# The second layer's order written out by hand, without arithmetic on GpSimd and with its weight units fetched sixteen ahead

## The chip, the cores and the metric

The kernel runs on one core of one Trainium2 chip. The metric is the device time of one execution in microseconds (us), as the median of several executions.

The names used below are those of the profile: PE is TensorE, DVE is VectorE, ACT is ScalarE, POOL is GpSimd, SP is SyncE, whose queue issues most DMAs.

## What is computed

Memory attention over 4 batches of 576 tokens and 8 heads (softmax over the sequence, 32 memory slots), then two feed-forward layers over the 2304 tokens. The change touches the border between the two layers and all of the second one.

```python
def _moe_ref(x, w_in, w_out):            # first layer: 512 -> 2048 -> 512
    h = np.maximum(x @ w_in, 0.0)
    return (h * h @ w_out).astype(np.float32)

def _moe2_ref(x, w_in, w_out):           # second layer: 512 -> 2048 -> 512
    h = x @ w_in
    sp = np.where(h > 20.0, h, np.log1p(np.exp(np.minimum(h, 20.0))))
    g = h * np.tanh(sp)                  # "mish"
    return (g @ w_out).astype(np.float32)

def reference(**kwargs):
    ...
    x = np.ascontiguousarray(attn_out.transpose(0, 2, 1, 3)).reshape(B * S, H * D)
    x = _moe_ref(x=x, **moe_kwargs)
    return _moe2_ref(x=x, **moe2_kwargs)
```

## The kernel before

**Arithmetic.** Each float32 operand is split in a high part (a cast to fp32r on ACT) and a low part (the rest, by a subtraction on DVE), and a product is three matmuls: high by high, low by high, high by low. The second layer's two products are done 2 by 2 in blocks with seven block products instead of eight, which needs sums of blocks on both sides: sums of weights, made once and stored in DRAM as "units" (`wf`, 256 KB each), and sums of activations, made beside the matmuls.

**Weight sums.** The class `Fold` makes the units out of the raw weights. For each 128 rows an exponent step on ACT (L275, Prelu) and two bit steps on DVE (L291, L293; `fields`) rebuild the float32 number; for each pair of row groups seven steps (`pair`) make sums on DVE, a cast on ACT (L310), a subtraction on DVE (L311) and a write from POOL's queue to `wf` (L312). The staging buffers of these writes come from `fold.stage`. This goes on beside the first layer, a step or two at each call of `fold.tick`, and the last nine casts run beside the first steps of the second layer, one at each step, with five staging buffers (three in the pool `cv`, two in `cs`).

**Border.** The last tile of the first layer (`a_tile`, L241 to L629) runs its second matmul group (`mm2_step`, L568 to L570) three steps late. After it, `flush()` makes the last `g` operand (cast L622 and subtraction L623 on DVE) and `run_pend(0)` runs the last three such groups, then copies the sums out (L585, L587) and stores them.

**Second layer.** Tokens go in three groups of 768. In each group there are 56 "h" steps (`h_step`: 8 row groups `k` by 7 products `j`) and 56 "b" steps (`b_step`: 7 products by 8 `k`); each is six matmuls of 384 columns that use one unit. In an h step, PSUM goes to SBUF by a copy on ACT (j=0) or an add on DVE (L1034, L1042, L1045), and Mish runs on ACT (L1030). For the b steps `cast_step` makes the high part (ACT, L1068) and the low part (DVE, L1069) of the operand, three steps ahead. Three sums are made on POOL: two for the operands (L1071, L1073, 128x384, 48 in all) and the sums of the next group's input (L918, L922, L925, L928 in `y_work`, 128x768, four for each of two groups). Four loads of the next group's input (L904) are at h steps 8 to 14.

**Units.** `feed` issues the loads of units from SP, in order. Unit n goes to one of 8 buffers, so that it can be issued once unit n-8 has been used; from unit 56 on there are 16 buffers.

**Order.** The tile framework orders each engine's instructions by its own estimate of times, within the dependences and within a few orderings given by hand (`behind`, L141). So DVE, ACT and PE mix steps of the second layer with the end of the first one, and POOL's sums go where the planner puts them.

Of the kernel before, what the change touches and what calls it, by code (L numbers as in the profile page):

```python
# [38 lines left out]
def body(tc, q, kvm, kvt, phi, w_in1, w_out1, w_in2, w_out2, out):  # L39
# [108 lines left out]

    class Conv:
# [86 lines left out]
    class Fold:  # L236
# [32 lines left out]

        def work(self, start, pops):  # L270
            todo, self.bits = self.bits, []
            if start and self.started < self.loaded and len(self.steps) < 5 and self.landed():
                key, u = self.order[self.started]
                high = self.raw[key, u][:, :, 1].bitcast(F32)
                nc.scalar.activation(high, high, AF.Prelu, scale=2.0 ** -112, alpha=-2.0 ** 32)  # L275
                self.started += 1
                self.bits.append((key, u))
# [618 lines left out]
    def y_work(i, raw, tmp):  # L896
# [16 lines left out]
        sub = nc.vector.tensor_sub if i == 0 else nc.gpsimd.tensor_sub  # L913
# [13 lines left out]
        def sum4():  # L927
            sub(r[1, 0], r[1, 0], r["t2"])  # L928
# [4 lines left out]
        if i:  # L933
# [3 lines left out]
                lambda: cast(2, r[0, 1]), lambda: (cast(4, r[1, 0]), sum4()),  # L937
# [40 lines left out]
    assert not y0  # L978
    flush()
    run_pend(0)  # L980
# [31 lines left out]
    def h_step(i, k, j, banks, tmp, g):  # L1012
# [7 lines left out]
        for d in range(2):  # L1020
# [5 lines left out]
            nc.tensor.matmul(ps, wl, yh[:, d], start=False, stop=end, **kw)  # L1026

# [4 lines left out]
        def total(name, a):  # L1032
            t = half_tile("hs", f"hs{m}", 3)
# [3 lines left out]
        if j == 0:  # L1037
            tmp["t"] = half_tile("ht", f"ht{m}", 2)
            nc.scalar.copy(tmp["t"], ps)
        elif j == 1:  # L1040
            tmp["u2"] = half_tile("hu2", f"hu2{m}", 2)
            add(tmp["u2"], tmp["t"], ps)  # L1042
        elif j == 2:
            tmp["u3"] = half_tile("hu3", f"hu3{m}", 2)
# [19 lines left out]
    def cast_step(j, k, g):  # L1064
        x = g[k, OPER[j]]
        hi, lo = ops[j, k] = tuple(
            G.tile([P, HT], F32R, tag=f"op{part}", name=f"op{part}{now}", bufs=5) for part in "hl")
        marks["hi"] = nc.scalar.copy(hi, x)  # L1068
        marks["lo"] = sub(lo, x, hi.bitcast(F32))  # L1069
        if j == 0:  # L1070
            at(k, lambda: nc.gpsimd.tensor_sub(x, g[k, "x1"], x))  # L1071
        elif j == 4:
            at(k, lambda: nc.gpsimd.tensor_sub(x, x, g[k, "a11"]))  # L1073

    def b_step(i, j, k, banks, tmp):
# [8 lines left out]
        for d in range(2):  # L1084
            ps = banks[role][d][:, :HT]
            wh, wl = (w[:, s, d * P:d * P + P] for s in range(2))
            first, end = k == 0 and j < 4, k == NPG - 1
            nc.tensor.matmul(ps, wh, hi, start=first, stop=False, **kw)  # L1088
            nc.tensor.matmul(ps, wl, hi, start=False, stop=False, **kw)  # L1089
            nc.tensor.matmul(ps, wh, lo, start=False, stop=end, **kw)  # L1090
        if k < NPG - 1:
            return

        def each(f, *ts, of=role):
            for d in range(2):
                f(*(t[:, d] for t in ts), banks[of][d][:, :HT])
# [4 lines left out]
        def store(t, a, b):  # L1101
            c0 = i * TT + a * HT
            nc.sync.dma_start(
                out[b * 256:b * 256 + 256, c0:c0 + HT].rearrange("(d p) t -> p d t", p=P), t)

        if j == 0:
            tmp["t"] = big("bt")
            each(nc.scalar.copy, tmp["t"])
        elif j == 1:
            tmp["u2"] = big("bu2")  # L1110
# [101 lines left out]
```

## Time and profile before

| | us |
|---|---|
| median of 3 executions | 760.62 (760.58 to 760.94) |
| profiled execution | 760.09 |
| its span, first to last instruction | 758.3 |
| first matmul of the second layer | 381.25 |
| last matmul's start | 754.04 |

The profile is one execution on the one core. Times of rows are in us from the span's start. PE is pipelined: a matmul of 384 columns is shown with about 0.34 us and the next one starts 0.174 us later, so the distance between starts tells the pace.

### The profile page before, as it was taken

To read this page: it belongs to the slowest core of one execution; us is meant where nothing else is said; L and a number is where in the kernel's file an instruction comes from. 1 tells how busy PE (TensorE), PEld (TensorE's weight loads), DVE (VectorE), ACT (ScalarE), POOL (GpSimd) and SP (SyncE) were. 2 spreads that over 40 slices of the span, in tenths; PEclk is the share of its full clock that TensorE was granted. 3 is DMA by queue.
4 is the path that set the end of the run, shared out by engine and by line. 5 is a ranking of instruction groups with operands and counts; after the bars stand their busy time and mean duration, and the time that the engine had idled before them with its cause. 6 is when DMAs were issued, how large, how long until landed. Compare 5 with 4: busy or idle time off the path is not lost. (4 is left out here: it accounts for less than half of the span.)

```text
span 758.3 us, 15324 instructions
## 1 busy us (share of the span) xinstructions
PE 728.6 (96%) x5480; PEld 691.1 (91%) x5480; DVE 529.9 (70%) x1072; ACT 425.1 (56%) x960; POOL 131.1 (17%) x176
## 2 busy tenths in 40 slices
PE   5699999999999999999998999999999999999997
PEld 4487898999888898999998999989999989999997
DVE  3979936436697779778979746884746794656584
ACT  3677856656558587766845435652334652334552
POOL 0000000001112123233225201230411050111040
PEclk8699999999999999999999999999999999999999
DMA  9994704107888779679879889888987888787882
GB/s 336 404 409 171 246 32 140 56 30 257 315 310 310 272 280 332 230 273 303 298 254 365 277 259 355 253 251 277 332 270 251 251 256 286 242 265 237 267 263 83
DMA packets 87756, 195.27 MB, mean 258 GB/s; under 512 B 9856, under 2 KB 21120, under 8 KB 87680
## 3 DMA queue, kind: packets, MB, share of 16 engines
q1 hardware_dynamic: 78720, 164.92, 65.0%
q0 software_dynamic: 8960, 29.37, 9.9%
q8 instruction: 44, 0.72, 0.4%
q14 instruction: 32, 0.26, 0.1%
HBM read 151.26 MB, written 42.99 MB: 256 GB/s over the span
## 5 line engine op out<-in xcount | busy, mean ns | idle before, releaser
L568 PE MATMUL a<-g,o1h 128*128 128x288 f32 x512 | 149.2, 299 | 0.7 <-ACT g L620 0.5
L569 PE MATMUL a<-g,o1l 128*128 128x288 f32 x512 | 148.4, 297 | 0.0
L570 PE MATMUL a<-g,o1h 128*128 128x288 f32 x512 | 132.2, 295 | 0.1
L1069 DVE TENSOR_TENSOR opl<-a,oph 128x384 fp32r<-128x384 f32 x144 | 92.9, 664 | 44.4 <-ACT oph L1068 43.8
L1024 PE MATMUL hb<-ych,u 128*128 128x384 f32 x336 | 113.8, 339 | 3.2 <-DVE hs L1034 1.8
L1025 PE MATMUL hb<-ycl,u 128*128 128x384 f32 x336 | 113.7, 338 | 0.0
L1026 PE MATMUL hb<-ych,u 128*128 128x384 f32 x336 | 110.9, 338 | 0.0
L1068 ACT CAST oph<-a 128x384 fp32r<-128x384 f32 x144 | 73.9, 513 | 61.2 <-PE b22acc L1089 8.0
L568 PEld LDWEIGHTS a<-g,o1h 128*128 128x128 f32 x512 | 96.3, 189 | 5.2 <-ACT s L614 2.1
L569 PEld LDWEIGHTS a<-g,o1l 128*128 128x128 f32 x512 | 96.5, 189 | 0.8 <-issue 0.8
L614 ACT ACTIVATE s<-h 128x288 f32<-128x288 f32 x128 | 52.7, 411 | 74.0 <-PE h L608 66.9
L570 PEld LDWEIGHTS a<-g,o1h 128*128 128x128 f32 x512 | 89.7, 188 | 3.8 <-issue 1.5
L1030 ACT ACTIVATE a<-hs 128x384 f32<-128x384 f32 x72 | 37.6, 525 | 98.1 <-DVE hs L1034 98.1
L606 PE MATMUL h<-ah,wp 128*128 128x288 f32 x256 | 78.9, 309 | 4.8 <-ACT wp L497 2.8
L623 DVE TENSOR_TENSOR g<-s,g 128x288 fp32r<-128x288 f32 x128 | 57.7, 451 | 34.6 <-ACT g L620 33.2
L312 POOL DMA_DIRECT2D wf_i<-st x56 | 30.7, 550 | 272.6 <-DVE st L311 257.1
L608 PE MATMUL h<-ah,wp 128*128 128x288 f32 x256 | 76.1, 297 | 0.7 <-DVE wp L498 0.7
L607 PE MATMUL h<-al,wp 128*128 128x288 f32 x256 | 76.4, 299 | 0.3 <-DVE al L481 0.3
L1034 DVE TENSOR_TENSOR hs<-hu,hb 128x384 f32<-128x384 f32 x72 | 39.6, 552 | 42.9 <-PE hb L1026 42.5
L1024 PEld LDWEIGHTS hb<-ych,u 128*128 128x128 f32 x336 | 63.6, 189 | 3.8 <-DVE hs L1034 2.1
L1025 PEld LDWEIGHTS hb<-ycl,u 128*128 128x128 f32 x336 | 63.5, 189 | 0.0
L1026 PEld LDWEIGHTS hb<-ych,u 128*128 128x128 f32 x336 | 63.4, 189 | 0.0
(277 smaller groups left out, 1559.1 us busy)
## 6 DMA issues: line engine op xcount, KB each, us to landing
u<-wf_i SPq DMA_DIRECT2D x168, 256.0 KB, 3.9
u<-wf_o SPq DMA_DIRECT2D x168, 256.0 KB, 3.3
raw_i<-in_moe_w_in_dram SPq DMA_DIRECT2D x32, 512.0 KB, 5.6
raw_o<-in_moe_w_out_dram SPq DMA_DIRECT2D x32, 512.0 KB, 6.8
wf_i<-st POOLq DMA_DIRECT2D x56, 256.0 KB, 4.8
wf_o<-st POOLq DMA_DIRECT2D x56, 256.0 KB, 4.6
win1r<-w_i SPq DMA_DIRECT2D x16, 512.0 KB, 5.3
kv<-in_kvm_dram SPq DMA_DIRECT2D x5, 1024.0 KB, 8.7
```

Of the source, the lines that this page charges most:

```text
L568: nc.tensor.matmul(o, wh[:, c, cs], sh, start=first, stop=False)
L569: nc.tensor.matmul(o, wl[:, c, cs], sh, start=False, stop=False)
L570: nc.tensor.matmul(o, wh[:, c, cs], sl, start=False, stop=last)
L606: nc.tensor.matmul(ph, w[:, 0, hg, fs], hi[:, hg], start=(hg == 0), stop=False)
L607: nc.tensor.matmul(ph, w[:, 0, hg, fs], lo[:, hg], start=False, stop=False)
L608: nc.tensor.matmul(ph, w[:, 1, hg, fs], hi[:, hg], start=False, stop=(hg == 1))
L623: marks["lo"] = nc.vector.tensor_sub(sl, s, sh.bitcast(F32))
L1024: nc.tensor.matmul(ps, wh, yh[:, d], start=(j < 4 and d == 0), stop=False, **kw)
L1025: nc.tensor.matmul(ps, wh, yl[:, d], start=False, stop=False, **kw)
L1026: nc.tensor.matmul(ps, wl, yh[:, d], start=False, stop=end, **kw)
L1068: marks["hi"] = nc.scalar.copy(hi, x)
L1069: marks["lo"] = sub(lo, x, hi.bitcast(F32))
```

## The change

A context manager `written` is added. Between its entry, just before the `flush()` at the border, and its exit after the last step, every instruction of PE, DVE and ACT is put behind the one traced before it on the same engine. So these three engines follow the order of the source. SP's and POOL's queues are not bound by it. In that order:

- All outstanding exponent steps (L275) and the load of Mish's activation table come first on ACT, then the rest of the first layer, then the h steps. The two bit steps that are left run at steps 3 and 5, and the pending steps of `pair` at every second step from step 7 on. The two extra staging buffers (`cs`) are gone, so these writes share three.
- Units 16 to 23, 32 to 39 and so on use eight more buffers (`ru2`); `feed` runs at the end of a step and goes up to 16 units ahead from step 16 on, two units at each step from 8 to 15.
- In the first group the loads of the next input are at steps 22 to 28 and its sums at 34, 39 and 44.
- Sums on POOL go to DVE: `x2` (in the h steps) and `x4` (`FOURTHS`), and `y_work`'s four sums.
- Temporaries share one tag `w` of 13 buffers; casts run four steps ahead in place of three; casts of the next input sit at `CASTS`.
- At the end of a b product each half is copied out and stored by itself (128 rows), the first half before the matmuls of the second.

```diff
+    @contextlib.contextmanager
+    def written(*engines):
+        traced = nc.cur_bb.bb.instructions
+        last = {x.engine: x for x in traced}
+        seen = traced[-1]
+        yield
+        start = next(k for k in reversed(range(len(traced))) if traced[k] is seen) + 1
+        for x in traced[start:]:
+            if x.engine not in engines:
+                continue
+            if x.engine in last:
+                tc.add_manual_dep(
+                    x, last[x.engine].name,
+                    mybir.DependencyInfo(mybir.DependencyClass.NoSync, mybir.DependencyReason.DATA),
+                    reason="written")
+            last[x.engine] = x
...
+        def start(self):
+            key, u = self.order[self.started]
+            high = self.raw[key, u][:, :, 1].bitcast(F32)
+            nc.scalar.activation(high, high, AF.Prelu, scale=2.0 ** -112, alpha=-2.0 ** 32)
+            self.started += 1
+            self.bits.append((key, u))
...
-        sub = nc.vector.tensor_sub if i == 0 else nc.gpsimd.tensor_sub
+        sub = nc.vector.tensor_sub
...
-            pool, tag = (G, "ru2") if n >= 56 and n % 2 else (Y2, "ru")
+            pool, tag = (G, "ru2") if n >= 16 and n // 8 % 2 == 0 else (Y2, "ru")
...
+    layer2 = written(mybir.EngineType.PE, mybir.EngineType.DVE, mybir.EngineType.Activation)
+    layer2.__enter__()
     flush()
+    extra[0] = None
+    while fold.started < fold.cap:
+        fold.start()
+    nc.scalar.preload_act_table_set("mish")
+    late, fold.bits = fold.bits, []
     run_pend(0)
...
-    cm_cs, CS = open_pool("cs", "right")
-    def stage_cs(n):
-        pool, tag, bufs = (CS, "stg2", 2) if n % 5 in (1, 3) else (CV, "stg", 3)
-        return pool.tile([P, 2, 256], F32R, tag=tag, name=f"st{n}", bufs=bufs)
-    fold.stage = stage_cs
...
+            def second():
+                g[k, "x2"] = half_tile(f"x2_{k}", f"x2{i}{k}", 1)
+                sub(g[k, "x2"], g[k, "x1"], g[k, "a11"])
             at(3, sums)
+            at(5, second)
-    OPER = ["a11", "a11", "a21", "x1", "a12", "a22", "a12"]
+    OPER = ["a11", "x2", "a21", "x1", "a12", "a22", "x4"]
...
-        if j == 0:
-            at(k, lambda: nc.gpsimd.tensor_sub(x, g[k, "x1"], x))
-        elif j == 4:
-            at(k, lambda: nc.gpsimd.tensor_sub(x, x, g[k, "a11"]))
+    def fourth(k, g):
+        x = g[k, "x4"] = g.pop((k, "a11"))
+        sub(x, g[k, "a12"], g[k, "x2"])
...
-    AHEAD = 3
+    AHEAD = 4
+    CASTS = (4, 10, 15, 20, 22, 27, 36, 42)
+    FOURTHS = (7, 12, 17, 25, 29, 38, 40, 44)
...
     for now, (kind, i, one, two) in enumerate(plan):
-        feed(now + (8 if now < 56 else 16))
...
+        if kind == "h":
+            if i == 0 and late and step in (3, 5):
+                fold.fields(*late.pop(0))
+            elif i == 0 and fold.steps and step > 6 and step % 2:
+                assert step < 40
+                fold.steps.pop(0)()
+            if step == 0 and more:
+                loads, sums, casts = y_work(i + 1, in_g("yr", 4), in_g("yt", 2))
+            if more and step in ((22, 24, 26, 28) if i == 0 else (8, 10, 12, 14)):
+                loads.pop(0)()
+            if more and step in ((34, 39, 44) if i == 0 else (24, 29, 34)):
+                sums.pop(0)()
+        else:
+            if more and step in CASTS:
+                casts.pop(0)()
+            if step in FOURTHS:
+                fourth(FOURTHS.index(step), g)
+        next(part, None)
+        feed(now + 9 if now < 8 else min(now + 17, 2 * now + 2))
+    layer2.__exit__(None, None, None)
```

## Rows read from the trace of the kernel before

**Rows 1.** The page, part 1: busy time (share of the span) and instructions by engine.

```profile
PE 728.6 (96%) x5480; PEld 691.1 (91%) x5480; DVE 529.9 (70%) x1072; ACT 425.1 (56%) x960; POOL 131.1 (17%) x176
```

**Rows 2.** Busy time by window; after POOL: granted PE clock, DMA share, GB/s.

```profile
410.00:420.00 10.00, 6.81 (x32) 6.17 (x32) 10.00 (x14) 3.24 (x7) 7.26 (x9) 0.90 1.03 400
```

**Rows 3.** Waits of PE in the b steps: who for whom, us in total, times, longest.

```profile
PE b02acc L1090 <- DVE opl L1069: 1.0, 2, 0.5
PE b12acc L1090 <- DVE opl L1069: 1.0, 2, 0.5
```

**Rows 4.** Timeline of PE in the first h steps: start, duration, instruction, idle before.

```profile
410.86 0.34 PE L1026 MATMUL hb<-ych,u 128*128 128x384 f32 x1
412.62 0.44 PE L1024 MATMUL hb<-ych,u 128*128 128x384 f32 x1 [1.42 <-DMA u<-wf_i]
...
415.70 0.34 PE L1026 MATMUL hb<-ych,u 128*128 128x384 f32 x1
417.80 0.48 PE L1024 MATMUL hb<-ych,u 128*128 128x384 f32 x1 [1.77 <-DVE hs L1034]
...
421.56 0.34 PE L1024 MATMUL hb<-ych,u 128*128 128x384 f32 x1
```

**Rows 5.** Timelines of DVE and POOL ahead of the second of these gaps.

```profile
411.61 3.76 DVE L1058 TENSOR_TENSOR a<-a,a 128x384 f32<-128x384 f32 x1
...
411.33 1.83 POOL L922 TENSOR_TENSOR yt<-yr,yt 128x768 f32<-128x768 f32 x1
413.10 1.85 POOL L925 TENSOR_TENSOR yr<-yr,yr 128x768 f32<-128x768 f32 x1
```

**Rows 6.** Timelines of PE and DVE in the first group's b steps.

```profile
494.35 0.41 PE L1090 MATMUL b00mm<-opl,u 128*128 128x384 f32 x1
...
501.61 0.34 PE L1088 MATMUL b02acc<-oph,u 128*128 128x384 f32 x1
...
493.72 5.23 DVE L1069 TENSOR_TENSOR opl<-a,oph 128x384 fp32r<-128x384 f32 x4
```

**Rows 7.** Timelines of PE and DVE at the border of the layers.

```profile
381.25 0.34 PE L1024 MATMUL hb<-ych,u 128*128 128x384 f32 x1
...
390.81 0.34 PE L1025 MATMUL hb<-ycl,u 128*128 128x384 f32 x1
...
394.57 0.29 PE L570 MATMUL a<-g,o1h 128*128 128x288 f32 x1
394.70 0.34 PE L1026 MATMUL hb<-ych,u 128*128 128x384 f32 x1
...
390.41 0.45 DVE L623 TENSOR_TENSOR g<-s,g 128x288 fp32r<-128x288 f32 x1
```

**Rows 8.** DMA issues, median us to landing: first two from 398 to 418, last from 425.

```profile
u<-wf_i SPq DMA_DIRECT2D x16, 256.0 KB, 5.9
wf_o<-st POOLq DMA_DIRECT2D x6, 256.0 KB, 5.8
...
u<-wf_i SPq DMA_DIRECT2D x22, 256.0 KB, 3.1
```

**Rows 9.** One weight sum's cast, subtraction and write; a short DVE sum; all writes' landing, 398 to 425.

```profile
398.70 0.41 ACT L310 CAST st<-ct_o 128x256 fp32r<-128x256 f32 x1 [3.38 <-DMA y<-ys]
399.14 0.42 DVE L311 TENSOR_TENSOR st<-ct_o,st 128x256 fp32r<-128x256 f32 x1 [2.92 <-ACT st L310]
399.86 0.54 POOL L312 DMA_DIRECT2D wf_o<-st  x1 [4.97 <-DVE st L311]
407.69 0.55 DVE L1057 TENSOR_TENSOR x<-a,a 128x384 f32<-128x384 f32 x1
...
DMA to landing us min/median/max: 2.8/5.6/6.2
```

**Rows 10.** Timeline at the end of the span: DVE's last two adds.

```profile
753.89 1.08 DVE L1096 TENSOR_TENSOR bo<-bu,b23acc 128x384 f32<-128x384 f32 x2 [3.74 <-PE b23acc L1090]
```

More of the change, by code (lines that the diff above doesn't have):

```diff
@@ L272, in work @@
             if start and self.started < self.loaded and len(self.steps) < 5 and self.landed():
[L273 to L277, printed above, removed]
+                self.start()
             for key, u in todo:
@@ L927, in sum4 @@
         def sum4():
-            sub(r[1, 0], r[1, 0], r["t2"])
+            if i:
+                sub(r[0, 0], r[1, 0], r["t2"])
+                r[1, 0] = r[0, 0]
+            else:
+                sub(r[1, 0], r[1, 0], r["t2"])
         sum1 = t1, lambda: cast(0, r[0, 0])
@@ L936, in y_work @@
             return work, sums, last + [
-                lambda: cast(2, r[0, 1]), lambda: (cast(4, r[1, 0]), sum4()),
+                lambda: cast(2, r[0, 1]), lambda: cast(4, r[1, 0]), sum4,
                 lambda: cast(6, r[1, 1]), lambda: cast(5, r[1, 0])]
@@ L1066, in cast_step @@
         hi, lo = ops[j, k] = tuple(
-            G.tile([P, HT], F32R, tag=f"op{part}", name=f"op{part}{now}", bufs=5) for part in "hl")
+            G.tile([P, HT], F32R, tag="w", name=f"op{part}{now}", bufs=13) for part in "hl")
         marks["hi"] = nc.scalar.copy(hi, x)
         marks["lo"] = sub(lo, x, hi.bitcast(F32))
-        if j == 0:
-            at(k, lambda: nc.gpsimd.tensor_sub(x, g[k, "x1"], x))
-        elif j == 4:
-            at(k, lambda: nc.gpsimd.tensor_sub(x, x, g[k, "a11"]))
+    def fourth(k, g):
+        x = g[k, "x4"] = g.pop((k, "a11"))
+        sub(x, g[k, "a12"], g[k, "x2"])
     def b_step(i, j, k, banks, tmp):
@@ L1083, in b_step, with big, store @@
         kw = dict(skip_group_check=True)
+        ends = k == NPG - 1
+        def big(tag, bufs=1):
+            return big_pool[0].tile([P, 2, HT], F32, tag=tag, name=f"{tag}{m}", bufs=bufs)
+        def store(t, d, a, b):
+            c0 = i * TT + a * HT
+            r0 = b * 256 + d * P
+            nc.sync.dma_start(out[r0:r0 + P, c0:c0 + HT], t[:, d])
+        if ends and j in (0, 1, 2):
+            tmp[j] = big(("bt", "bu2", "bu3")[j])
+        if ends and j in (2, 4, 5, 6):
+            t = big("bo", 3)
         for d in range(2):
@@ L1086, in b_step @@
             wh, wl = (w[:, s, d * P:d * P + P] for s in range(2))
-            first, end = k == 0 and j < 4, k == NPG - 1
+            first = k == 0 and j < 4
             nc.tensor.matmul(ps, wh, hi, start=first, stop=False, **kw)
             nc.tensor.matmul(ps, wl, hi, start=False, stop=False, **kw)
[L1090 to L1096, printed above, removed]
-        def big(tag, bufs=1):
-            return big_pool[0].tile([P, 2, HT], F32, tag=tag, name=f"{tag}{m}", bufs=bufs)
[L1101 to L1110, printed above, removed]
-            each(add, tmp["u2"], tmp["t"])
-        elif j != 3:
-            t = big("bo", 3)
+            nc.tensor.matmul(ps, wh, lo, start=False, stop=ends, **kw)
+            if d == 0:
+                yield
+            if not ends or j == 3:
+                continue
+            if j == 0:
+                nc.scalar.copy(tmp[0][:, d], ps)
+            elif j in (1, 2):
+                add(tmp[j][:, d], tmp[j - 1][:, d], ps)
             if j == 2:
-                tmp["u3"] = big("bu3")
-                each(add, tmp["u3"], tmp["u2"])
-                each(add, t, tmp["u3"], of=3)
+                add(t[:, d], tmp[2][:, d], banks[3][d][:, :HT])
             elif j == 4:
-                each(nc.scalar.copy, t)
-            else:
-                each(add, t, tmp["u2"])
-            store(t, *{2: (1, 1), 4: (0, 0), 5: (1, 0), 6: (0, 1)}[j])
+                nc.scalar.copy(t[:, d], ps)
+            elif j in (5, 6):
+                add(t[:, d], tmp[1][:, d], ps)
+            if j in (2, 4, 5, 6):
+                store(t, d, *{2: (1, 1), 4: (0, 0), 5: (1, 0), 6: (0, 1)}[j])
     plan = []
@@ L1138, in body @@
         if kind == "h":
-            h_step(i, one, two, banks, tmp, g)
-            if i == 0 and fold.busy():
-                assert step < 40
-                fold.tick(pops=1, took=0.43)
-            if step == 0 and more:
-                loads, sums, casts = y_work(i + 1, in_g("yr", 4), in_g("yt", 2))
-            if more and 8 <= step < 16 and step % 2 == 0:
-                loads.pop(0)()
-            if more and step in (24, 29, 34):
-                sums.pop(0)()
+            part = h_step(i, one, two, banks, tmp, g)
         else:
             if now == 56:
-                close(cm_cs)
                 close(cm_cv)
                 cm_bo, big_pool[0] = open_pool("bo", "right")
-            b_step(i, one, two, banks, tmp)
-            if more and 18 <= step < 46 and step % 4 == 2:
-                casts.pop(0)()
+            part = b_step(i, one, two, banks, tmp)
+        next(part)
         run_queue()
```

10 lines of the change are left out of this document (6 added, 4 removed).

## The prediction

> **What bounds the kernel now.** I read the engine table first: PE is busy 96% of the span and no other engine is over 70% [rows 1]. So time is to be had only where PE loses its pace, and an engine beside it matters only where it makes PE late. Matmuls of the second layer follow each other at 0.174 us; 3 groups of 112 steps of 6 make 2016 of them, or 351 us. A step is 1.04 us. Busy time by window then finds the one bad stretch: from 410 to 420 PE has 32 matmuls in place of 57, at a granted clock of 0.90, with DVE busy all the time and the DMA engines saturated [rows 2]. The waits of PE name two more, in the b steps of the first two groups [rows 3]. Last come the timelines, for what each loss is. There are three kinds.
>
> The first is a unit that lands late: at 410.86 the next matmul comes 1.76 us later, and the one behind it 0.28 later, which loses 1.59 + 0.10 = 1.7 us [rows 4]. Units land there 5.9 us after their issue, against 3.1 us in a calm stretch [rows 8], and a unit is issued seven steps, 7.3 us, before its use at the most. The four loads of the next input (384 KB each) and the weight writes crowd this stretch.
>
> The second is DVE: at 415.70 PE waits for an add, 2.10 us from start to start, so 1.93 lost, and then 12 matmuls from 417.80 to 421.56 take 3.76 us instead of 2.09, another 1.67, at the lower of the two clock levels [rows 2, 4]. Total 3.6 us. The add is late because DVE's queue is: one subtraction of 128x384 took 3.76 us, until POOL's two sums of 1.83 and 1.85 beside it were over [rows 5]; the same kind of operation takes 0.55 us where POOL is idle [rows 9].
>
> The third is the same thing in the b steps: four low-part subtractions take 5.23 us, and the 26 matmuls from 494.35 to 501.61 take 7.26 us instead of 4.52 [rows 6]: 2.7 us lost. The second group has its twin, with waits of the same lengths [rows 3]; the third has none, as no next input is summed there. So 5.4 us.
>
> Together 1.7 + 3.6 + 5.4 = 10.7 us. That is the most that order and prefetch can bring, apart from the end.
>
> **Part by part.** *POOL's arithmetic* is taken away, so the second and third kinds have no cause: minus 9.0 us. What it costs: DVE gets 48 subtractions of 128x384 at 0.47 us (the distance of back-to-back ones; 0.55 is the shown duration [rows 9]) and eight sums of 128x768, by twice the columns some 0.93 us each (an estimate): 23 + 7 = 30 us in 351. DVE is at 70% of the span with its blocked operations counted [rows 1], so it has room on the whole. The narrowest place is steps 20 to 31 of the b part: 12 low parts, two casts of the next input and one sum, two `x4`, and six adds out of PSUM come to 12 x 0.47 + 3 x 0.93 + 8 x 0.47 = 12.2 us in 12.5. That is full, but casts now run four steps (4.2 us) ahead, which covers the unevenness. In the h steps PE needs each sum two steps after its product, 2.1 us; a burst of two short sums and one add is 1.4. I take nothing; the bounds are 0 and the whole 5.4 us that the b steps lost.
>
> *Units sixteen ahead, loads of the next input at steps 22 to 28*: the late unit goes, minus 1.7. Units 8 to 15 have the same seven steps of lead as before, but without the loads beside them; later ones have eight to sixteen steps. What is triggered: steps 8 to 15 fetch two units a step, 512 KB in 1.04 us or some 500 GB/s, where the saturated window moved 400 [rows 2]. The surplus queues up on SP and is worked off over the next 20 steps. The units can bear it by their lead; the first sum of the next input has some 10 us from its second load to its use against landings of 5.9 us and up, so it holds too. Who can't bear it are the weight writes.
>
> *Weight sums on three buffers, one each second step.* Nine casts go in three rounds of three buffers. One turn of a buffer is the cast 0.41, the subtraction 0.42, 0.30 until POOL issues, and the landing [rows 9]. Landings between 398 and 425 were 2.8 to 6.2 us [rows 9], median 5.8 while the DMA engines were saturated [rows 8]; I take 6.0, as the stretch will be at least as full. With the handovers that is 7.1 us, and three buffers at one cast in 2.09 us give 6.27. So the second and the third round each fall 0.85 us behind. In the written order this is no longer off the path: ACT waits for the buffer, DVE's subtraction waits for ACT, and the adds that free PSUM for PE are behind it in the same queue, with little to spare because DVE's work of these steps fills most of its slack. I put all of it on PE: plus 1.7 us. Bounds: 0 for landings up to 5.1 us, and 5.7 if they rise to 8.
>
> On these landings the Trainium skill (DMA: Bandwidth & Descriptors, "Anatomy of one DMA") has a fit for DMAs from GpSimd's queue, 2.0 us plus bytes over 436 GB/s, which for 256 KB is an estimate of 2.6 us; by it a turn is 3.7 us, nothing waits, and the sum would be 1.7 us lower (the first rival below). The rows say 5.8 in this stretch and only the calm minimum, 2.8, comes near it, so I keep the rows.
>
> *The border.* Before, PE did 20 matmuls of the second layer between 381.25 and 390.81, while the first layer waited for `g` on DVE, and went on with the second layer alone at 394.70 [rows 7]. Counted back, the second layer started at 394.70 - 20 x 0.174 = 391.2. In the written order it starts after the first layer's last group. DVE is saturated here with work that the change doesn't touch, and its last `g` subtraction starts at 390.41 and ends at 390.86 [rows 7]; 12 matmuls at 0.133 us (394.57 to 394.70 [rows 7]) follow, so the second layer starts at 392.5: plus 1.3 us. Bounds: 0 if DVE's queue turns out better sorted, and 3.5 if none of the 20 is made up for; if the gaps lower the clock as at 417.80, 1.7 more. The exponents and the table load on ACT are hidden: the first copy that PE waits for is due four steps into the second layer.
>
> *The end.* The last adds start at 753.89 and take until 754.97 [rows 10], and the store is issued behind both. By halves the first is out 0.5 us earlier and the last one is smaller: minus 0.2, bounds 0 and minus 0.5.
>
> *Thirteen shared temporaries* and the order itself: a cast's buffer was last used six steps ago, so no wait; nothing.
>
> **The sum.** -10.7 + 1.7 + 1.3 - 0.2 = -7.9. The profiled execution took 760.09 us, 0.5 below the median 760.62, with 1.8 us outside its span; the same difference off the median gives **752.7 us**.
>
> **Rivals.** (a) *The weight writes cost nothing*, because they land in under 5.1 us: 752.7 - 1.7 = 751.0. For it: the calm landings. Against it: this stretch gets fuller. (b) *The border is dear*: none of the 20 matmuls is made up for (2.2 more) and the lower clock follows (1.7 more): 756.6. For it: PE sat behind DVE here and the exponents now stand in a fixed place on ACT, where one of them waits for its data. Against it: a single gap of 1.76 us did not change the clock [rows 4]. (c) *The change does half of what it says*: with 30 us more on DVE the low parts of the b steps stay late, and 5.4 us come back: 758.1. Against it: DVE needs 12.2 of 12.5 us at its worst. (d) *Slower*: the two units a step hold the weight writes up so long that three buffers rule the first 25 steps. Each microsecond of landing over 5.1 costs 2; the gain of 10.7 - 1.3 + 0.2 = 9.6 is gone at a landing of 9.9 us, and at 11 the time is 752.7 + 10.0 = 762.7. Against it: no landing there was over 6.2 [rows 9].
>
> **Chances.** Forecast 0.50, (a) 0.23, (b) 0.14, (c) 0.07, (d) 0.06. A difference of 0.2%, 1.5 us, is about what a measurement of this kernel can tell from none. Forecast, (a), (b) and more than half of (c) are faster by more: 0.88; the rest of (c) and the edge of (d) are the same: 0.06; slower 0.06. The range goes from (a) with its bounds at the end and at the border, 749.8, to (b) with a microsecond on it, 757.6.
>
> **What will show it.** On DVE, no operation of 128x384 over 0.6 us from 400 on, and no POOL sums; no wait of PE for low parts at the places of rows 6; no wait for a unit at step 18. At the border no matmul of the second layer before the last L570, and its first one at about 392.5. ACT's L310 waiting for a write to land, and PE waiting for DVE between steps 15 and 27, by 1.7 us in all. What would make the prediction wrong: a wait of PE in the b steps, a longer stop at the border, or a stretch of lower clock behind it.

## The result and the profile after

The changed kernel takes 752.56 us (median of 4 executions, 751.68 to 753.22); beside it on the same chip the kernel before took 760.6. The ratio is 0.9891 [0.9876, 0.9906]. The profiled execution took 752.62 us with a span of 750.8, against 758.3 before: 7.5 us less. The forecast was 752.7.

First the two rows that answer to [rows 1, 2]. The engine table of the changed kernel:

```profile
PE 724.9 (97%) x5480; PEld 689.9 (92%) x5480; DVE 525.7 (70%) x1128; ACT 419.3 (56%) x960; POOL 62.0 (8%) x120
```

The 56 sums went from POOL to DVE, and yet DVE is busy 4 us less: by this row the blocked time that it lost is more than the work that it got. Busy time by window (the column behind POOL is PE's granted clock, then DMA share and GB/s):

```profile
410.00:420.00 10.00, 8.04 (x46) 7.59 (x45) 7.08 (x16) 3.72 (x9) 2.17 (x4) 1.00 1.05 407
```

The stretch that had 32 matmuls at a clock of 0.90 now has 46 at full clock. 11 of the 57 are still missing, and the DMA engines are as full as before. All the waits of PE from 370 us to the end are these two (who waits for whom: us in total, times, longest):

```profile
PE hb L1050 <- DVE hu L1072: 2.0, 1, 2.0
PE a L591 <- DVE g L644: 1.3, 1, 1.3
```

(Lines moved: the h matmuls are now L1050 to L1052, the b matmuls L1134 to L1136, a weight sum's cast, subtraction and write L331, L332, L333, the low part of a cast step L1101, the `x2` and `x4` sums L1089 and L1105, and the adds out of PSUM L1061, L1069, L1072.) Nothing stands for [rows 3], and nothing for the late unit of [rows 4]. The DVE operations of [rows 5, 6] are back at their own length; here are two low parts with an `x4` sum between them, in the b steps where four low parts took 5.23 us, and the group of all such low parts (count, busy us, mean ns, idle before):

```profile
492.71 0.55 DVE L1101 TENSOR_TENSOR opl<-a,oph 128x384 fp32r<-128x384 f32 x1
493.18 0.55 DVE L1105 TENSOR_TENSOR a<-a,x 128x384 f32<-128x384 f32 x1
493.65 0.55 DVE L1101 TENSOR_TENSOR opl<-a,oph 128x384 fp32r<-128x384 f32 x1
...
L1101 DVE TENSOR_TENSOR opl<-a,oph 128x384 fp32r<-128x384 f32 x120 | 62.9, 554 | 22.6 <-ACT oph L1100 16.1 <-PE b21bg L1135 1.9 <-PE b22acc L1135 1.4
```

**The one big wait.** The timelines of PE, ACT, DVE and POOL around it:

```profile
411.69 0.34 PE L1052 MATMUL hb<-ych,u 128*128 128x384 f32 x1
413.98 0.44 PE L1050 MATMUL hb<-ych,u 128*128 128x384 f32 x1 [1.96 <-DVE hu L1072]
...
403.92 0.54 POOL L333 DMA_DIRECT2D wf_o<-st  x1 [1.69 <-DVE st L332]
411.06 0.42 ACT L331 CAST st<-raw_o 128x256 fp32r<-128x256 f32 x1 [1.66 <-DMA wf_o<-st]
...
411.51 0.43 DVE L332 TENSOR_TENSOR st<-raw_o,st 128x256 fp32r<-128x256 f32 x1 [3.04 <-ACT st L331]
411.85 0.55 DVE L1069 TENSOR_TENSOR hu<-ht,hb 128x384 f32<-128x384 f32 x1
412.32 0.55 DVE L1084 TENSOR_TENSOR x<-a,a 128x384 f32<-128x384 f32 x1
412.90 0.56 DVE L1085 TENSOR_TENSOR a<-a,a 128x384 f32<-128x384 f32 x1
413.38 0.55 DVE L1072 TENSOR_TENSOR hu<-hu,hb 128x384 f32<-128x384 f32 x1
```

It reads from the bottom up. PE waits for the add L1072; that add waited for nothing but its turn behind four operations; the first of these, the weight sum's subtraction, had DVE stand still for 3.04 us until ACT's cast was there; the cast waited for a staging buffer, whose write was issued at 403.92 and landed 7.06 us later, at 410.98. DVE had work for PE in its queue all that time, and the written order kept it behind the weight sum. A second, smaller one follows at 421.36 (0.48 from start to start). A third stop, 0.32 at 443.77, has another cause: a sum of the next input (L946, 0.95 us from 442.63 on) stands in DVE's queue between two short sums and the add that PE needs.

**The border**, timelines of PE and DVE:

```profile
391.87 0.30 PE L591 MATMUL a<-g,o1h 128*128 128x288 f32 x1
392.00 0.34 PE L1050 MATMUL hb<-ych,u 128*128 128x384 f32 x1
...
389.90 0.45 DVE L644 TENSOR_TENSOR g<-s,g 128x288 fp32r<-128x288 f32 x1
```

No matmul of the second layer runs before the first layer's last, as written. Where [rows 7] counted back gave a start 0.81 us after DVE's last `g` subtraction (391.22 against 390.41), it is now 2.10 us after it.

**Where the 7.5 us are.** From here on "the stretch" is the time from the second layer's start (matmuls that ran earlier counted back at 0.174 us each) to the start of the last matmul, and "lost" is the sum of all distances between matmuls in it beyond 0.174 (those beyond by less than 0.04 are left out). Before, the stretch was 362.82 with 10.62 lost; after, it is 354.75 with 2.97 lost (2.30 at 411 and the next step, 0.41 at 421, 0.26 at 444). That is 8.1 us gained, 7.65 of it lost pace and 0.42 from matmuls that follow a little closer. The border costs 1.3, the end gives 0.27 (4.29 to 4.02 us from the last matmul to the end of the span), and the first layer happened to end 0.5 us earlier. 8.1 - 1.3 + 0.3 + 0.5 = 7.6.

That last term is chance: over the kernels below, DVE's last `g` subtraction, which none of them means to touch, lay between 389.1 and 391.6 us in those with the border as the change has it. It moves the whole time by a microsecond or two. So the stretch and the lost pace, which come from one profile each, decide about a mechanism, and the times only about what is larger.

### The profile page after: what moved, and what is told of

Read it like the earlier page. It is cut to its first block, busy times and chain, and to the rows that moved or that the text cites. A ratio compares the mean times of both kernels' runs of the same rounds, so it can differ in the third digit from the quotient of the medians.

```text
span 750.8 us, 15294 instructions
## 1 busy us (share of the span) xinstructions
PE 724.9 (97%) x5480; PEld 689.9 (92%) x5480; DVE 525.7 (70%) x1128; ACT 419.3 (56%) x960; POOL 62.0 (8%) x120
## 4 chain that ended last, share of the span: by engine, by line
PE 70%; issue 13%; DVE 5%; DMA 5%; POOL 4%; ACT 3%; SPq 0%; POOLq 0%; ACTq 0%; DVEq 0%
PE hb L1050 7%; PE hb L1051 7%; PE hb L1052 7%; PE a L589 5%; PE a L591 5%; PE a L590 5%; POOL wf_o L333 3%; PE h L627 3%; PE h L629 2%; PE h L628 2%; DMA raw_i<-in_moe_w_in_dram 2%; DMA kv<-in_kvm_dram 1%; PE pw L512 1%; PE pk L428 1%; DMA wf_i<-st 1%
## 5 line engine op out<-in xcount | busy, mean ns | idle before, releaser
L1050 PE MATMUL hb<-ych,u 128*128 128x384 f32 x336 | 113.5, 338 | 2.1 <-DVE hu L1072 2.0
L1052 PE MATMUL hb<-ych,u 128*128 128x384 f32 x336 | 113.1, 336 | 0.0
L1100 ACT CAST oph<-a 128x384 fp32r<-128x384 f32 x120 | 59.4, 512 | 37.9 <-PE b22acc L1136 7.4
L1101 DVE TENSOR_TENSOR opl<-a,oph 128x384 fp32r<-128x384 f32 x120 | 62.9, 554 | 22.6 <-ACT oph L1100 16.1
L1050 PEld LDWEIGHTS hb<-ych,u 128*128 128x128 f32 x336 | 63.0, 188 | 3.2 <-DVE hu L1072 3.0
L1052 PEld LDWEIGHTS hb<-ych,u 128*128 128x128 f32 x336 | 63.0, 188 | 0.0
L627 PEld LDWEIGHTS h<-ah,wp 128*128 128x128 f32 x256 | 48.2, 189 | 14.9 <-ACT s L635 4.5
L1061 DVE TENSOR_TENSOR hs<-hu,hb 128x384 f32<-128x384 f32 x72 | 39.7, 553 | 26.1 <-PE hb L1052 24.3
```

What stands on the lines that cost most here:

```text
L627: nc.tensor.matmul(ph, w[:, 0, hg, fs], hi[:, hg], start=(hg == 0), stop=False)
L1050: nc.tensor.matmul(ps, wh, yh[:, d], start=(j < 4 and d == 0), stop=False, **kw)
```

## The experiments

Each kernel is the changed kernel with the edit shown, but for the one that starts from the kernel before. The kernel before took 759.80, 759.56 and 760.22 us in the three sets they were run in. The changed kernel once more, as the measure for the others:

> The changed kernel once more, unchanged, so that the three beside it are compared on one chip. The second layer, from its start (counted back over matmuls done early) to its last matmul, took 354.75 us in the first profile, with 2.97 us of lost pace in it; both theories expect that within 0.3 us, as the landings of the weight writes may differ a little. What comes ahead of the border moved by 1 to 2 us from run to run, so the stretch is read, not the span alone.

754.05 us, ratio 0.9932 [0.9914, 0.995]; stretch 354.06, lost 2.24. The same three stops: 1.74 us at 411.77 (2.29 the first time), 0.31 at 420.88, 0.32 at 443.12. The stretch is 0.7 us shorter than the first time, where 0.3 was expected at most: the landing that the cast waits for took 6.51 us in place of 7.06. So the size of the wait at the staging buffer varies with a landing, its place does not. The two ratios of this one kernel, here and in the result, differ by more than their intervals, so an interval tells nothing of what differs from set to set.

**1. Is it the turn of the three staging buffers?** Two ways: five buffers at the same pace, or three at a slower pace (one weight sum at each third step, from 7 to 31).

```diff
+    def stage_g(n):
+        if n % 5 in (1, 3):
+            return G.tile([P, 2, 256], F32R, tag="yt", name=f"st{n}", bufs=2)
+        return CV.tile([P, 2, 256], F32R, tag="stg", name=f"st{n}", bufs=3)
+    fold.stage = stage_g
```

> The changed kernel with two more staging buffers for the weight writes (five in place of three, the two taken from a tag that is not used before step 34); nothing else is different. Theory of the turn: in the changed kernel PE waited 2.3 us at 411.7 and 0.4 us at 421.4 because ACT waited for a weight write to land (7.06 us) before it could fill the third buffer again; with five buffers a turn may take 5 x 2.09 = 10.4 us, every landing seen fits, both waits go, and the time falls by 2.7 us, from 752.6 to 749.9. Rival: the waits come from the sums and bit steps that now stand in DVE's queue in a fixed order, whatever the buffers; then the waits stay and the time stays at 752.6 within 0.5.

```diff
-            elif i == 0 and fold.steps and step > 6 and step % 2:
+            elif i == 0 and fold.steps and step > 6 and step % 3 == 1:
```

> The changed kernel with one weight sum each third step in place of each second (steps 7 to 31 in place of 7 to 23), three buffers as in the changed kernel. Theory of the turn: three buffers at one cast in 3.13 us give 9.4 us a turn, over the 7.1 to 8.2 us that a turn took; the two waits of PE go as with five buffers: 749.9 to 750.3. Rival (DVE's queue is too full): the same work spread thinner helps as well, but five buffers don't; so this run and the run with five buffers agree by the theory of the turn and differ by the rival.

Five buffers: 751.43 us, 0.9898 [0.987, 0.9925], stretch 352.63, lost 0.79. Each third step: 751.18 us, 0.9884 [0.9862, 0.9906], stretch 352.08, lost 0.26. Waits of ACT from 396 to 425 us, of the changed kernel first, and then, as the only one left, of that with five buffers:

```profile
ACT a L1057 <- DVE hs L1061: 15.3, 11, 3.7
ACT st L331 <- DMA wf_o<-st: 4.3, 3, 1.7
```

```profile
ACT a L1064 <- DVE hs L1068: 17.8, 11, 3.7
```

With no wait for a buffer the stop at 411 shrinks from 2.29 us to 0.52 (five) or is gone (third step), and the one at 421 is gone in both. The stretch gets 1.4 to 2.7 us shorter than in the two runs of the changed kernel. That the turn of the buffers was the price in the h steps is shown by both ways; the 0.52 us left with five buffers has another cause, which stays open. The whole times can't tell: the ratios 0.9898 and 0.9884 lie beside the two of the changed kernel, 0.9891 and 0.9932, which was not run in this set.

**2. Do the two units fetched at each step hold up the weight writes?** `feed` is held to one unit a step:

```diff
-        feed(now + 9 if now < 8 else min(now + 17, 2 * now + 2))
+        feed(now + 9)
```

> The changed kernel with units fetched eight ahead all along, one at each step, in place of two at each of steps 8 to 15 and sixteen ahead. Theory of the crowded DMA engines: without the surplus of 500 GB/s the weight writes land in 4 to 5 us in place of 5.3 to 7.1, a turn of a buffer is under 6.3 us, and PE's waits near 411 and 421 (2.2 to 2.7 us) go: the second layer takes 352.0 to 352.5 us in place of 354.1 to 354.8. The units have seven steps of lead and land in 3 to 5 us, so PE does not wait for them, except beside the four loads of the next input, where landings over 7.3 us would show as a wait for a unit. Rival: the landings stay at 5.5 to 7 because the writes themselves and POOL's path set them; the waits stay.

753.68 us, 0.9919 [0.9889, 0.9949], stretch 353.84, lost 2.02. How long the nine writes from 398 to 425 us took to land, here, in the repeated changed kernel and in its first profile:

```profile
DMA to landing us min/median/max: 5.6/5.7/5.9
...
DMA to landing us min/median/max: 3.8/5.9/6.5
...
DMA to landing us min/median/max: 5.3/5.6/7.1
```

The typical write lands as slowly without the surplus, against the 4 to 5 us that were expected. PE's two waits for the add stay (1.16 us at 412.02, 0.66 at 420.57), and no unit is late. The slowest landing is less, 5.9 us against 6.5 and 7.1, and so is what PE loses at the two stops: 1.76 us against 1.98 and 2.71. So the surplus is not the reason for landings near 6 us; whether it makes the slowest one slower, one profile can't show. Sixteen units ahead are not needed: eight do, in the written order and with the loads moved.

**3. What do the moved loads and sums bring alone?** The kernel before, with the loads of the next input at steps 22 to 28 and its sums at 34, 39 and 44 in the first group:

```diff
-            if more and 8 <= step < 16 and step % 2 == 0:
+            if more and step in ((22, 24, 26, 28) if i == 0 else (8, 10, 12, 14)):
...
-            if more and step in (24, 29, 34):
+            if more and step in ((34, 39, 44) if i == 0 else (24, 29, 34)):
```

> The kernel before with one part of the change alone: the loads of the next input of the first group at steps 22 to 28 and their sums at 34, 39 and 44. Theory: the wait for a unit (1.7 us at 410.9) goes; POOL's sums meet DVE at another place, so the wait of 2.1 us at 415.7 and the stretch of lower clock move or go, and the b steps keep their 2.7 us in each of two groups: 757 to 759, against 760 of the kernel before. Rival: eight units ahead are too few anyway, as the weight writes crowd the stretch; the wait for a unit stays, 760.

757.21 us, 0.9963 [0.9948, 0.9978], stretch 359.28, lost 7.12. Waits of PE and, from DVE's timeline, the one long operation beside POOL's sums of 128x768:

```profile
PE hb L1024 <- DMA u<-wf_i: 1.1, 2, 0.6
PE b12acc L1090 <- DVE opl L1069: 1.0, 2, 0.5
PE b02acc L1090 <- DVE opl L1069: 1.0, 2, 0.5
...
431.12 2.09 DVE L1057 TENSOR_TENSOR x<-a,a 128x384 f32<-128x384 f32 x1 [0.59 <-ACT a L1030]
```

Of the 10.6 us lost before, the move alone takes 3.5. Of the 5.3 in the h steps 1.8 are left: the unit is late by 0.95 and 0.78 us from start to start, with the eight buffers of the kernel before, and DVE's operation beside POOL's sums takes 2.09 us where it took 3.76 [rows 5]; no wait of PE comes of it there, and no slow clock. That the unit is late still was not expected. The 2.7 us in each of the two groups' b steps stay whole.

**4. What was POOL's arithmetic worth?** First all 56 sums back on POOL, with POOL's own queue free; then with POOL in the written order too:

```diff
-        sub = nc.vector.tensor_sub
+        sub = nc.vector.tensor_sub if i == 0 else nc.gpsimd.tensor_sub
...
-                sub(g[k, "x2"], g[k, "x1"], g[k, "a11"])
+                nc.gpsimd.tensor_sub(g[k, "x2"], g[k, "x1"], g[k, "a11"])
...
-        sub(x, g[k, "a12"], g[k, "x2"])
+        nc.gpsimd.tensor_sub(x, g[k, "a12"], g[k, "x2"])
```

> The changed kernel with all of the sums that were moved to DVE (x2, x4, the four sums of the next input) issued on POOL again, at the same places of the source; order, units and casts as in the changed kernel. Theory of the shared queue: DVE's operations beside POOL's sums take 1 to 4 us again, the low parts come late and PE waits in the b steps of the first two groups, 1 to 2.7 us in each, and in h steps: 755 to 759. Rival: written order and casts four steps ahead did away with the waits, and where the sums run does not matter: 752.6 within 0.5.

```diff
-    layer2 = written(mybir.EngineType.PE, mybir.EngineType.DVE, mybir.EngineType.Activation)
+    layer2 = written(mybir.EngineType.PE, mybir.EngineType.DVE, mybir.EngineType.Activation, mybir.EngineType.Pool)
```

> The kernel with the sums back on POOL (769.2 us), with POOL in the written order too, so that its sums run where they are written and not at the start of the b steps. Theory of the shared queue: each sum of 1.0 us on POOL still holds up DVE's operation beside it by 0.5 to 2 us, but they are spread out as in the changed kernel; PE waits are 3 to 10 us in all: 755 to 762. Rival: the 769 came from the sums' place alone (POOL ran them in a bunch while DVE made low parts); spread out they cost nothing, 752.6.

769.22 us, 1.0124 [1.0093, 1.0154], stretch 370.61, lost 18.93; and 768.54 us, 1.0139 [1.0115, 1.0162], stretch 368.85, lost 17.06. Both are slower than the kernel before, and by far more than was expected. From the first, the largest waits of PE (one in the b steps of each group), and timelines of PE, DVE and POOL before the first of them:

```profile
PE b10mm L1136 <- DVE opl L1101: 2.0, 1, 2.0
PE b20mm L1136 <- DVE opl L1101: 2.0, 1, 2.0
PE b00mm L1136 <- DVE opl L1101: 2.0, 1, 2.0
...
463.98 0.44 PE L1136 MATMUL b00mm<-opl,u 128*128 128x384 f32 x1 [1.96 <-DVE opl L1101]
...
460.00 1.37 DVE L1084 TENSOR_TENSOR x<-a,a 128x384 f32<-128x384 f32 x1
461.40 1.25 DVE L1085 TENSOR_TENSOR a<-a,a 128x384 f32<-128x384 f32 x1
462.58 1.81 DVE L1101 TENSOR_TENSOR opl<-a,oph 128x384 fp32r<-128x384 f32 x2
...
459.76 2.48 POOL L1105 TENSOR_TENSOR a<-a,x 128x384 f32<-128x384 f32 x2 [1.00 <-DVE opl L1101]
462.20 1.30 POOL L1089 TENSOR_TENSOR x<-x,a 128x384 f32<-128x384 f32 x1
```

DVE's short operations, 0.55 us alone, take 1.25 and 1.37 beside POOL's of 1.24 to 1.30: the two engines go in step. The engine table of this kernel tells what the help is worth:

```profile
PE 733.5 (96%) x5480; PEld 693.3 (90%) x5480; DVE 520.0 (68%) x1072; ACT 419.3 (55%) x960; POOL 135.8 (18%) x176
```

POOL takes 56 operations off DVE, 74 us of its own time, and DVE's busy time falls from 525.7 to 520.0 (523.8 with POOL in the order), not by the 30 us that the prediction counted for them. The Trainium skill (SBUF — State Buffer, "Who interferes with whom") says that DVE and GpSimd share one pair of ports under an exclusive lock; these rows agree. With the same 56 sums on POOL the kernel before lost 10.62 us, and these two lose 18.93 and 17.06; that a DVE queue which may not be reordered hands more of the delays on to PE is the likely reason, but casts and the places of the sums differ too, so it is not shown. The third group, which sums no next input, has the wait as well, so in this order the short sums are enough for it. To see the other share, the four sums of the next input alone on POOL, on top of the weight sums at each third step:

```diff
-        sub = nc.vector.tensor_sub
+        sub = nc.vector.tensor_sub if i == 0 else nc.gpsimd.tensor_sub
```

> The kernel with one weight sum each third step, with only the four sums of the next input (eight in all, 128x768) back on POOL; x2 and x4 stay on DVE. Of the 15 to 16 us that all sums on POOL cost, this tells which: if the share goes by POOL's time, 8 x 1.85 = 15 of 63 us, so 4 us; if x2 and x4 with their chain through POOL are the cause, under 1.5 us; if the long sums are, over 8 us. The second layer of the kernel beside it takes 352.1 us. The theory of the shared queue by the kernel before's rows (a DVE operation waits out the sum beside it) expects 1 to 4.

752.54 us, 0.9903 [0.9874, 0.9932], stretch 354.20, lost 2.42, against 352.08 and 0.26. One stop of 2.49 us, at 434.27; nothing in the b steps. Timelines of DVE and POOL:

```profile
432.01 2.15 DVE L1084 TENSOR_TENSOR x<-a,a 128x384 f32<-128x384 f32 x1
434.19 2.05 DVE L1085 TENSOR_TENSOR a<-a,a 128x384 f32<-128x384 f32 x1
...
431.91 1.84 POOL L943 TENSOR_TENSOR yt<-yr,yt 128x768 f32<-128x768 f32 x1 [0.73 <-DMA u<-wf_i]
433.70 2.13 POOL L946 TENSOR_TENSOR yr<-yr,yr 128x768 f32<-128x768 f32 x1
```

This is the picture of [rows 5] again, in another place. So the long sums alone are worth 2.1 us, and they cost PE nothing in the b steps. The rest of the 14.1 to 16.5 us between the changed kernel's two profiles and the two with all sums on POOL, 12 to 14 us, comes with the 48 short ones, alone or beside the long ones: with POOL in the written order, the b steps of the third group, which have short sums alone, lose 2.9 us, and those of the first two groups, with the next input's last sum and casts among them, 5.7 each. The short sums alone on POOL were not run.

In the kernel before this was otherwise. Its third group has the same short sums on POOL in its b steps and loses nothing; in the first two, the next input's last sum and casts stand among them. POOL's timeline in the first group, then DVE's and POOL's in the third:

```profile
493.88 2.08 POOL L928 TENSOR_TENSOR yr<-yr,yt 128x768 f32<-128x768 f32 x1 [0.89 <-DVE ycl L911]
...
732.55 7.17 DVE L1069 TENSOR_TENSOR opl<-a,oph 128x384 fp32r<-128x384 f32 x9
...
733.41 3.79 POOL L1073 TENSOR_TENSOR a<-a,a 128x384 f32<-128x384 f32 x3 [0.56 <-DVE opl L1069]
```

Nine low parts in 7.17 us, single ones of 1.37 among them, and PE doesn't wait for any.

**5. The border.** PE, DVE and ACT are left to the framework until the first h step, and in another kernel the whole second layer is:

```diff
-        last = {x.engine: x for x in traced}
+        last = {}
...
-    layer2.__enter__()
     flush()
...
+    layer2.__enter__()
     for now, (kind, i, one, two) in enumerate(plan):
```

> The changed kernel with the written order beginning at the first h step and not tied to what was traced before it: the end of the first layer is left to the framework, which mixes matmuls of the second layer into it as in the kernel before. Theory: the border costs 1.3 us in the changed kernel (one gap of 1.6 us at 381.5 and one of 0.3), which the mixed matmuls fill: 752.6 - 1.3 = 751.3. Rival: DVE holds the first layer's end in any order, and what PE does earlier it waits for later; 752.6 within 0.5.

```diff
-    layer2 = written(mybir.EngineType.PE, mybir.EngineType.DVE, mybir.EngineType.Activation)
+    layer2 = contextlib.nullcontext()
```

> The changed kernel without the written order: the framework orders all engines as in the kernel before; sums on DVE, prefetch, buffers and places in the source as in the changed kernel. Theory of the border: the framework mixes matmuls of the second layer into the first layer's end, so that the second layer's start, counted back over the matmuls done early, is 0.8 us after DVE's last g subtraction begins, as in the kernel before, in place of 2.1. With the sums off POOL the b steps lose nothing. Then the whole is 1.3 us below the changed kernel if the weight writes cost the same, or some us above if the framework's order of casts is worse. Rival: the border's cost is in DVE's saturated queue and not in PE's order; 2.1 stays.

For these the second layer's start is measured from the sixth `g` subtraction from the end, which lies before anything the edits move: 8.09 us in the kernel before, 9.37 and 9.42 in the two runs of the changed kernel. That is the 1.3 us again. (DVE's last `g` subtraction, the anchor of the expectations, comes later itself in the two kernels here.)

Border free: 754.25 us, 0.993 [0.9906, 0.9954], stretch 354.50, lost 2.63; 15 early matmuls, but a start of 10.00. On ACT an exponent now stands ahead of the first layer's Relus and waits for its data, and DVE's last `g` is 1.4 us later for it:

```profile
386.36 0.67 ACT L291 ACTIVATE raw_o<-raw_o 128x512 f32<-128x512 f32 x1 [4.76 <-DMA raw_o<-in_moe_w_out_dram]
```

All free: 755.81 us, 0.9942 [0.9922, 0.9962], stretch 356.24, lost 4.12; 24 early matmuls and a start of 9.11, as DVE's last `g` again comes 1.35 us later, and again an exponent on ACT waits for its data, 3.81 us. So neither kernel shows what the border alone is worth. The waits of PE in the second one show what the written order is worth in the h steps:

```profile
PE hb L1050 <- ACT ht L1066: 1.5, 3, 0.5
PE hb L1050 <- DMA u<-wf_i: 1.3, 1, 1.3
```

A unit is late again, by 1.64 us from start to start, and in each group one copy on ACT comes late, 0.8 us lost with what follows. The b steps lose nothing. So without the written order the stretch is still 6.6 us shorter than before (362.82 to 356.24), by the sums on DVE, the prefetch and the places together; the written order adds 1.5 to 2.2 us, with the stops at the staging buffers in it.

**6. A better one?** The third sum of the next input two steps later, with weight sums at each third step; and then PE alone untied at the border, with DVE and ACT in the written order throughout (`tied=False` begins PE's order at the first h step, without the first layer's last matmul ahead of it):

```diff
-            if more and step in ((34, 39, 44) if i == 0 else (24, 29, 34)):
+            if more and step in ((34, 39, 46) if i == 0 else (24, 29, 34)):
```

> The changed kernel with one weight sum each third step and the third sum of the next input at step 46 in place of 44 (44 is the step in which two short sums and an add stand in DVE's queue too). Theory: the lost pace of the second layer goes from 2.97 to under 0.1 us, as 2.7 came from the turn of the buffers and 0.26 from the sum at step 44; time 2.9 us below the changed kernel beside it. Rival: the 0.26 us at 443.8 come from the landing of the next input and stay.

```diff
-    layer2 = written(mybir.EngineType.PE, mybir.EngineType.DVE, mybir.EngineType.Activation)
+    layer2 = written(mybir.EngineType.DVE, mybir.EngineType.Activation)
...
+    steps2 = written(mybir.EngineType.PE, tied=False)
+    steps2.__enter__()
     for now, (kind, i, one, two) in enumerate(plan):
...
+    steps2.__exit__(None, None, None)
     layer2.__exit__(None, None, None)
```

> As the kernel with one weight sum each third step and the sum at step 46, but PE alone is left free at the border: its h steps follow the written order among themselves and are not tied to the first layer's matmuls, while ACT and DVE keep the changed kernel's order. In the earlier run that freed all three engines, an exponent stood before a Relu on ACT and waited 4.76 us for its data, so it did not show the border by itself. Theory: the border's gaps of 1.6 and 0.3 us are filled by mixed matmuls, and the second layer starts 1.3 us earlier against DVE's last g subtraction (0.8 us after its start, as in the kernel before, in place of 2.1): 1.3 us below the kernel with three steps. Rival: matmuls of the second layer stand in PE's queue before the first layer's and hold them up, nothing is won.

The first: 752.11 us, 0.9901 [0.9885, 0.9916], stretch 352.14, lost 0.30. The stop at 443 is gone, as it should be, but an equal one is at 435.45, from the first sum of the next input, which waits for its load and pushes on the add behind it, and through that add's Mish and a copy on ACT the add that PE waits for:

```profile
431.30 0.96 DVE L939 TENSOR_TENSOR yt<-yr,yr 128x768 f32<-128x768 f32 x1 [1.28 <-DMA yr<-y]
```

The second: 751.34 us, 0.9891 [0.9875, 0.9906], beside 754.05 for the changed kernel in the same set. No matmul of the stretch of 351.82 us is late any more (the same sum waits 0.88 us there, which does no harm). The start is at 9.14, 0.25 better than the change, with 15 early matmuls, where 1.3 was expected: most of the border's price stays. It is the fastest of its set and has nothing left to gain within the stretch at this pace. What is left is the border.

## Why the prediction was right, step by step

- *The late unit, -1.7*: gone, as said. But the edit it was put down to wasn't needed in full: with eight ahead none is late either (experiment 2), with the moved loads alone and eight buffers some are (experiment 3). The buffers don't do it by themselves: without the written order a unit is late in spite of them (experiment 5). Whether the order would do without them was not tried.
- *The late add, -3.6, and the low parts, -5.4*: both gone, and experiment 4 brings them back by giving POOL its sums again. And without the written order, with the sums on DVE, the b steps lose nothing either (experiment 5). The two losses have different owners, which the prediction didn't tell apart: the sums of 128x768 made the first (2.1 us in experiment 4, without the slow clock that followed before). The second took both: the long sums alone on POOL cost nothing in the b steps (experiment 4, with casts four steps ahead), and the short sums alone cost nothing in the third group of the kernel before, as the prediction said of it. In the changed kernel's order the short ones alone are enough. DVE at 12.2 of 12.5 us was wide enough: PE doesn't wait once in the b steps. Rival (c) is out.
- *The weight writes, +1.7*: right in mechanism and place, ACT for a buffer, DVE for ACT, PE for the add behind it. The size was 2.7 us in the first profile and 2.0 in the second (the stops at 411 and 421 with the matmuls just after). The mis-sized term is the landing: 6.0 us was taken for all, near the median (5.6 before [rows 9], and 5.6 after). But here it was the slowest one that was paid: 7.06 us, with 0.41 + 0.42 + 0.30 for the rest of the turn 8.2 us (8.31 from one subtraction on that buffer, at 403.20, to the next, at 411.51) against the 6.27 that the pace allows, 1.9 late, and PE stood 1.96. Nor did the two rounds cost 0.85 each: the first stop was 2.30 us and the second 0.41. Where all nine landings lay between 5.6 and 5.9, in experiment 2, the two stops cost 1.76 us, which is the prediction's 1.7; so the mechanism holds and the landing is the term. Its reason was also wrong in part: landings near 6 us are not due to the two units at a step (experiment 2). Rival (a) is out: landings of 5.3 to 7.1 us are twice the 2.6 us that the Trainium skill's fit gives (DMA: Bandwidth & Descriptors, "Anatomy of one DMA"), and by the fit, with the turn of 3.7 us that the prediction made of it, no wait would have been seen.
- *A burst of two short sums and one add, 1.4 us in 2.1, nothing*: missed by one operation. At step 44 a sum of 128x768 joins the burst, another 0.87 us from start to start, 2.3 in all, and PE loses 0.26. The working had counted the sums of the next input in the b part only.
- *The border, +1.3*: measured 1.3, by both anchors, and in detail: the prediction put the second layer 12 matmuls of 0.133 us behind the end of the last `g` subtraction; from 390.35 that gives 391.95, and it is 392.00. Rival (b) is out. Why the framework's order had these 1.3 us and no variant with the change's other parts has them stays open: freeing all engines moves ACT's exponents and makes `g` late, freeing PE alone gives 0.25.
- *The end, -0.2*: measured -0.27.
- *No slow clock*: right, at 1.00 behind the 2.29 us stop. But see the last section: it need not have been.
- Two figures beside the sum don't add up as they stand: (a) with its bounds at the border and the end is 751.0 - 1.3 - 0.3 = 749.4, not 749.8, and the chances of being faster by more than 1.5 us are 0.91 by the parts named, not 0.88. Neither changes the forecast.

So the median fell 0.1 us from the forecast partly by luck: the weight writes cost 1.0 more and the sum at step 44 another 0.26, and a pace slightly closer (0.4 us in the stretch, which no step of the prediction has) and a first layer 0.5 us earlier took most of that away. The repeat in another set, at 754.05, is as good a value of the same kernel.

## What to carry to other kernels

When every engine is put in one written order, look for operations in it that wait for something from outside, a staging buffer or a load, and price them at the slowest landing of the stretch, since whatever stands behind them pays; thinner spacing or two more buffers are cheap. The sums, the prefetch and their places brought most of the gain here, 6.6 of some 8 us in the stretch, without a written order. Sums and differences on POOL were hardly a relief for DVE where both ran at once: here 30 us of DVE's work, by the prediction's count, took 2 to 6 us off DVE's busy time, and made single operations late. Read single effects of a microsecond from the stretch that the edit touches, not from the whole time, when an earlier part of the kernel moves by as much.

## What the runs showed of the hardware

A stop of PE of some 2.3 us sometimes lowers its clock and sometimes doesn't. In the kernel with all sums on POOL, three equal stops (2.295, 2.313 and 2.298 us from start to start, in the b steps of the three groups) were followed by a granted clock of 1.00, 0.51 and 0.51, the last two being the lower level, 1.2 GHz, for ten matmuls or so at 0.32 us. Busy time by window right behind each of the three stops (granted clock behind POOL):

```profile
464.00:466.00 2.00, 2.00 (x11) 2.00 (x12) 2.00 (x3) 0.48 (x1) 1.94 (x2) 1.00 0.11 26
586.50:589.50 3.00, 3.00 (x10) 3.00 (x11) 3.00 (x3) 0.48 (x1) 2.46 (x2) 0.51 0.19 38
709.40:712.40 3.00, 3.00 (x11) 3.00 (x10) 3.00 (x4) 0.80 (x2) 2.07 (x2) 0.51 0.34 85
```

In the kernel before, a stop of 2.10 us was enough [rows 4]; in the changed kernel one of 2.29 was not, nor one of 2.49 in the kernel with the long sums alone on POOL (granted clock 1.00 behind both). What tells them apart wasn't tried; a stop of this size should be counted with up to 1.7 us more, as the prediction's bound did.
